# Attention and two MLPs: matmuls with the same stationary operand placed next to each other

## The chip, the cores and the metric

The kernel runs on one core of a Trainium2 chip. The metric is the device time in microseconds (us) of one execution. Matmuls run on TensorE (PE; its weight loads are shown as PEld). VectorE is DVE, ScalarE is ACT, GpSimd is POOL and SyncE is SP. A matmul holds one operand in the array, the stationary one, which a weight load brings there, and streams the other, the moving one, past it.

## The reference

2304 tokens go through top-k attention and then through two MLPs with the same shapes (512 to 2048 to 512) and other activations. Cut to what matters:

```python
def _attn_ref(q, k, v):              # 4 batches, 8 heads, 576 positions, 64 wide
    scores = scale * np.matmul(q, k.transpose(0, 1, 3, 2))
    kth = np.partition(scores, -32, axis=-1)[..., -32:-31]
    scores = np.where(scores >= kth, scores, -1000000000.0)
    attn = np.exp(scores - np.max(scores, axis=-1, keepdims=True))
    attn = attn / (np.sum(attn, axis=-1, keepdims=True) + 1e-09)
    return np.matmul(attn, v)

x = attn_out.transpose(0, 2, 1, 3).reshape(2304, 512)
h = x @ w_in;  y = (h - np.tanh(h)) @ w_out              # first MLP
h = y @ w_in2; g = np.where(h > 0, h, np.exp(np.minimum(h, 0)) - 1)
out = g @ w_out2                                         # second MLP
```

## The kernel before

The tokens are cut into 6 chunks (`ci`) of 384. The attention of a later chunk runs while the MLPs of an earlier one run, so PE has matmuls of both. For the attention, PE makes scores (L383, L384: two matmuls that share their stationary operand `u.qs`), ACT copies them out (L385), and DVE finds the 32nd largest of each row of 576 in four rounds: MAX8 (L406) finds eight, MATCH_REPLACE (L420) takes them out, and after the last round a mask (L427) is applied. PE then transposes the result (L448) and multiplies it with v (L470).

An MLP (`m` is 0 for the first and 1 for the second) goes over 16 f-tiles (`ft`), each 128 of the 2048 hidden features. Every float32 operand is split into a high and a low part, and a product is the sum of three: high by high, and high by low both ways.

- `first(ci, m, ft)` makes 12 matmuls into the bank `h` (L577): the stationary operand is one of four blocks (`kt`) of the high (`wi` 0) or low (`wi` 1) weights `wt`, the moving one `xh` or `xl`, 384 columns. For `m` 1 the same roles are played by `zh` and `zl`, and the first two f-tiles (`PARTED`) are made in two column parts, 256 and 128 wide. ACT makes `t` from `h` (L580; L582 and L583 for `m` 1). There are two `h` banks, so `first` of f-tile ft+2 waits until the gate has read the bank of f-tile ft.
- `gate` makes `g` from `h` and `t`, on DVE (L591 for `m` 1, L596 for most f-tiles of `m` 0), and splits it: ACT makes `gh`, POOL `gl` (both L148 and L149, in a helper).
- `second(ci, m, ft)` adds nine matmuls to the three `acc` banks (L613), one for each 128 tokens `t`: the stationary operand is `gh[t]` or `gl[t]`, the moving one the high or low weights, 512 columns.
- `between(ci)` is the turn from the first MLP to the second: for each 128 tokens ACT copies `acc` to `y` (L627), PE transposes it (L630), ACT makes `zh` (L632) and DVE `zl` (L633). `first` of the second MLP's f-tiles 0 and 1 follows at once.

Every engine works through its own queue in order. The order is fixed when the kernel is built: the Python code emits the steps tick by tick, so many rounds of the attention beside so many f-tiles, and a list scheduler then places each instruction by its priority and a simulated time. A change in one engine's order can thus move instructions on the others.

Of the kernel before, what the change touches and what calls it, by code (L numbers as in the profile page):

```python
# [106 lines left out]
def tile_topk_attention_two_mlps(  # L107
# [20 lines left out]
    def mlp_tile(shape, dt, **kw):  # L128
        if "open" in pools:
            opening.close()  # L130
            del pools["open"]
            pools["mlp"] = pool("mlp", 1)
        return pools["mlp"].tile(shape, dt, **kw)
# [23 lines left out]
    def bank(tag, name, bufs):  # L157
        if tag == "h":
            if "park" in pairs:
                turns.close()  # L160
                del pairs["park"]
                pairs["h"] = pool("ph", 1, PSUM)
            return pairs["h"].tile([P, 512], F32, tag=tag, name=name, bufs=bufs)
        return ps.tile([P, 512], F32, tag=tag, name=name, bufs=bufs)
# [401 lines left out]
    def first(ci, m, ft):  # L566
        n = SIZES[ci]
        xh, xl = x_tiles[ci] if m == 0 else z_tiles[ci]
        h = bank("h", f"h{ci}_{m}_{ft}", 2)[:, :n]
        wv = weights[ci, m, ft][:, 0].rearrange("p a (k c) -> p a k c", c=P)  # L570
        jobs = [(wi, xs, kt) for wi, xs in ((0, xh), (1, xh), (0, xl)) for kt in range(4)]
        if m == 0 and ft == 0:
            jobs.sort(key=lambda x: x[2])
        late = (n // P - 1) * P
        for cs in (slice(0, late), slice(late, n)) if m == 1 and ft < PARTED and late else (slice(0, n),):
            for a, (wi, xs, kt) in enumerate(jobs):
                nc.tensor.matmul(h[:, cs], wv[:, wi, kt], xs[:, kt, cs], start=(a == 0), stop=(a == len(jobs) - 1))  # L577
        t = mlp_tile([P, NMAX], F32, tag="t", name=f"t{ci}_{m}_{ft}", bufs=T_BUFS)[:, :n]
        if m == 0:
            nc.scalar.activation(t, h, AF.Tanh)  # L580
        else:
            nc.scalar.activation(t, h, AF.Relu, scale=-1.0)  # L582
            nc.scalar.activation(t, t, AF.Exp, scale=-1.0)  # L583
        parts[ci, m, ft] = h, t
# [17 lines left out]
    def second(ci, m, ft):  # L602
        nt = SIZES[ci] // P
        if ft == 0:
            acc[ci, m] = [bank(f"acc{t}", f"acc{ci}_{m}_{t}", 1) for t in range(nt)]
        wt = weights.pop((ci, m, ft))[:, 1]
        gh, gl = parts.pop((ci, m, ft))
        jobs = [(k, t) for k in range(3) for t in range(nt)]
        if ft == NF - 1:
            jobs.sort(key=lambda x: x[1])  # L610
        for k, t in jobs:
            gx, wi = ((gh, 0), (gh, 1), (gl, 0))[k]
            nc.tensor.matmul(  # L613
                acc[ci, m][t],
                gx[:, t * P : t * P + P],
                wt[:, wi],
                start=(ft == 0 and k == 0),
                stop=(ft == NF - 1 and k == 2),
            )
# [31 lines left out]
    def step_parts(i):  # L651

        ci, m, ft = steps[i]
        nxt = steps[i + 1] if i + 1 < len(steps) else None
        turn = m == 0 and ft == NF - 1
        early = nxt is not None and not turn

        def a():
            if early:
                first(*nxt)  # L660

        def b():
            if early:
                gate(*nxt)

        def c():
            second(ci, m, ft)
            if turn:
                between(ci)
                first(*nxt)  # L670
                gate(*nxt)
            if m == 1 and ft == NF - 1:
                store(ci)
            load_next()

        return a, b, c
# [54 lines left out]
    for tick in range(FIRST_TICK, n_ticks):  # L731
# [7 lines left out]
        if tick == starts[0]:  # L739
            first(*steps[0])  # L740
            gate(*steps[0])
# [71 lines left out]
```

## Time and profile before

| | |
|---|---|
| time, median of 3 runs | 1217.33 us (1217.17 to 1217.76) |
| time of the profiled execution | 1221.19 us |
| its span | 1219.4 us |
| busy in the span: PE, PEld | 1150.4 us (94%), 976.2 us (80%) |
| busy in the span: DVE, ACT, POOL | 950.1 us (78%), 764.1 us (63%), 503.1 us (41%) |
| matmuls, weight loads | 6349, 6349 |
| mean granted clock of PE | 0.972 of full speed |

The span is the stretch between the first and the last recorded instruction; the time of an execution also holds what lies around it. Rows of the trace and sums of them belong to the profiled execution.

### The profile page before, as it was taken

The page shows a single profiled execution, that of the slowest core. Times are in us where ns is not written, and L with a number is a line of the kernel's source. Part 1 is how long each engine was busy: PE and PEld are TensorE (multiplying, and loading weights), DVE is VectorE, ACT ScalarE, POOL GpSimd, SP SyncE. Part 2 cuts the span into 40 slices and gives each one's busy share as a digit, 9 for nine tenths or more (in the row PEclk, how much of TensorE's full clock was granted, in tenths as well). Part 3 has the DMA queues.
Part 4 walks back from the last instruction along what each step waited for, and adds up shares of the span by engine and source line. Part 5 has one row for each costly group of instructions (what it writes and reads, how often), then busy time and mean ns, then how long its engine had stood idle before and what let it go on. Part 6 is the DMA issues. An engine that isn't in the chain of part 4 may idle for free.

```text
span 1219.4 us, 18848 instructions
## 1 busy us (share of the span) xinstructions
PE 1150.4 (94%) x6349; PEld 976.2 (80%) x6349; DVE 950.1 (78%) x1896; ACT 764.1 (63%) x1592; POOL 503.1 (41%) x557
## 2 busy tenths in 40 slices
PE   6477789998999999999999999999999999999998
PEld 3344478887887978898988988988988988898897
DVE  7899999998999999789888779898789996100111
ACT  4999978988975546474564666575555564432333
POOL 2345348666752323253524444434434413333221
PEclk9688899998999999999999999999999999999999
DMA  7999728984989985759886779988679875686572
GB/s 233 361 354 336 241 73 295 365 288 142 385 345 290 288 302 144 246 162 315 251 187 206 238 239 247 226 243 271 218 248 221 205 154 207 210 285 247 195 270 95
DMA packets 81328, 299.59 MB, mean 246 GB/s; under 512 B 18768, under 2 KB 36048, under 8 KB 51664
## 3 DMA queue, kind: packets, MB, share of 16 engines
q1 hardware_dynamic: 81232, 298.39, 76.8%
q8 instruction: 50, 0.82, 0.3%
q14 instruction: 46, 0.38, 0.1%
HBM read 252.97 MB, written 45.39 MB: 245 GB/s over the span
## 4 chain that ended last, share of the span: by engine, by line
PE 58%; ACT 2%; DVE 1%; POOL 0%; issue 0%; ACTq 0%; POOLq 0%; DVEq 0%
PE acc L613 24%; PE h L577 24%; PE av L470 3%; PE pt L448 3%; PE ps L383 2%; PE ps L384 2%; DVE vm L406 0%; ACT y L627 0%; DVE w L420 0%; ACT zh L632 0%; ACT e L410 0%; ACT ph L449 0%; ACT s L385 0%; POOL kk L149 0%; ACT t L583 0%
## 5 line engine op out<-in xcount | busy, mean ns | idle before, releaser
L149 POOL TENSOR_TENSOR gl<-g,gh 128x384 fp32r<-128x384 f32 x192 | 203.4, 1061 | 371.8 <-ACT gh L148 352.3
L406 DVE MAX8 vm<-w 128x8 f32<-128x576 f32 x432 | 315.8, 748 | 3.2
L613 PE MATMUL acc<-wt,gh 128*128 128x512 f32 x1002 | 267.2, 398 | 0.3 <-ACT gh L148 0.3
L420 DVE MATCH_REPLACE8 w<-vm,w 128x576 f32<-128x576 f32 x288 | 212.8, 740 | 0.0
L613 PEld LDWEIGHTS acc<-wt,gh 128*128 128x128 f32 x1002 | 183.7, 188 | 33.9 <-issue 2.7
L148 ACT ACTIVATE gh<-g 128x384 fp32r<-128x384 f32 x192 | 100.6, 526 | 83.8 <-DVE g L591 43.3
L591 DVE SCALAR_TENSOR_TENSOR g<-t,h 128x384 f32<-128x384 f32 x96 | 52.4, 545 | 127.8 <-ACT t L583 127.4
L577 PE MATMUL h<-zh,wt 128*128 128x384 f32 (+2 forms) x768 | 145.8, 326 | 2.4 <-ACT zh L632 1.2
L613 PE MATMUL acc<-wt,gl 128*128 128x512 f32 x501 | 146.4, 398 | 0.0
L577 PE MATMUL h<-xh,wt 128*128 128x384 f32 x664 | 140.0, 339 | 2.0 <-DVE g L591 1.2
L448 PE MATMUL pt<-ident,e 128*116 128x128 f32 (+1 forms) x720 | 117.8, 290 | 20.2 <-ACT e L423 8.3
L385 ACT ACTIVATE s<-ps 128x288 f32<-128x288 f32 (+1 forms) x272 | 106.8, 416 | 45.2 <-PE ps L384 36.6
L406 DVE MAX8 vm<-s 128x8 f32<-128x576 f32 x144 | 107.4, 751 | 34.6 <-ACT s L385 32.6
L577 PEld LDWEIGHTS h<-zh,wt 128*128 128x128 f32 x768 | 124.9, 190 | 8.8 <-ACT zh L632 2.4
L449 ACT ACTIVATE ph<-pt 116x384 f32<-116x384 f32 (+1 forms) x240 | 111.2, 500 | 30.0 <-PE pt L448 29.5
L448 PEld LDWEIGHTS pt<-ident,e 128*116 128x116 f32 (+1 forms) x720 | 90.4, 143 | 43.2 <-ACT e L423 11.4
L577 PEld LDWEIGHTS h<-xh,wt 128*128 128x128 f32 x664 | 116.2, 188 | 9.0 <-DVE g L591 1.5
L582 ACT ACTIVATE t<-h 128x384 f32<-128x384 f32 x96 | 46.7, 488 | 108.2 <-PE h L577 108.0
L613 PEld LDWEIGHTS acc<-wt,gl 128*128 128x128 f32 x501 | 92.1, 188 | 18.5
L420 DVE MATCH_REPLACE8 w<-vm,s 128x576 f32<-128x576 f32 x144 | 106.6, 741 | 0.0
L580 ACT ACTIVATE t<-h 128x384 f32<-128x384 f32 x96 | 47.0, 491 | 90.9 <-PE h L577 90.8
L596 DVE TENSOR_TENSOR g<-h,t 128x384 f32<-128x384 f32 x76 | 41.4, 546 | 72.0 <-ACT t L580 71.5
(82 smaller groups left out, 1958.3 us busy)
## 6 DMA issues: line engine op xcount, KB each, us to landing
wt<-w SPq DMA_DIRECT2D x167, 1024.0 KB, 6.0
wr<-in_w_dram SPq DMA_DIRECT2D x32, 1024.0 KB, 8.9
w<-wp SPq DMA_DIRECT2D x32, 1024.0 KB, 8.4
kraw<-in_kT_dram SPq DMA_DIRECT2D x96, 144.0 KB, 5.4
vraw<-in_vL_dram SPq DMA_DIRECT2D x64, 160.0 KB, 5.2
sd<-sp SPq DMA_DIRECT2D x24, 288.0 KB, 5.8
s<-sd SPq DMA_DIRECT2D x24, 288.0 KB, 8.9
qraw<-in_qT_dram SPq DMA_DIRECT2D x64, 96.0 KB, 5.6
```

Source lines behind the costliest of these rows:

```text
L148: nc.scalar.activation(hi, src, copy)
L149: return nc.gpsimd.tensor_sub(lo, src, f(hi))
L385: nc.scalar.activation(s[lo:hi, cs], pt[lo:hi, :HS], copy)
L406: nc.vector.max(g.vm[:, j, min(r, 1)], u.s[t] if r == 0 else g.w[j])
L420: nc.vector.match_replace(g.w[j], v, u.s[t] if r == 0 else g.w[j], FILL)
L448: nc.tensor.transpose(pt[:kn, j * P : j * P + P], v.e[t][:, k0 : k0 + kn], ident)
L449: nc.scalar.activation(g.ph[:kn, blk, :nq], pt[:kn, :nq], copy)
L577: nc.tensor.matmul(h[:, cs], wv[:, wi, kt], xs[:, kt, cs], start=(a == 0), stop=(a == len(jobs) - 1))
L580: nc.scalar.activation(t, h, AF.Tanh)
L582: nc.scalar.activation(t, h, AF.Relu, scale=-1.0)
L591: nc.vector.scalar_tensor_tensor(g, t, -1.0, h, op0=ALU.add, op1=ALU.max)
L613: nc.tensor.matmul(acc[ci, m][t], gx[:, t * P : t * P + P], wt[:, wi], start=(ft == 0 and k == 0), stop=(ft == NF - 1 and k == 2),)
```

## The change

In `first`, the twelve matmuls of an f-tile are sorted so that the one with `xh` and the one with `xl` on the same block of high weights stand next to each other; the four on low weights come last. Before, the four with `xl` stood last. Only f-tile 0 of the first MLP had been sorted by `kt`. In `second`, `gh[t]` is used for the high and for the low weights in a row, and the three `gl` come last, as before; f-tile 15 already had the pairs.

```diff
         h = bank("h", f"h{ci}_{m}_{ft}", 2)[:, :n]
         wv = weights[ci, m, ft][:, 0].rearrange("p a (k c) -> p a k c", c=P)
-        jobs = [(wi, xs, kt) for wi, xs in ((0, xh), (1, xh), (0, xl)) for kt in range(4)]
+        jobs = [(wi, xs, kt) for wi, xs in ((0, xh), (0, xl), (1, xh)) for kt in range(4)]
         if m == 0 and ft == 0:
             jobs.sort(key=lambda x: x[2])
+        else:
+            jobs.sort(key=lambda x: (x[0], x[2]))
...
         jobs = [(k, t) for k in range(3) for t in range(nt)]
         if ft == NF - 1:
             jobs.sort(key=lambda x: x[1])
+        else:
+            jobs.sort(key=lambda x: (x[0] == 2, x[1]))
         for k, t in jobs:
             gx, wi = ((gh, 0), (gh, 1), (gl, 0))[k]
```

No instruction is added or taken away, and each engine has as many as before. Their order is another on every engine, because the scheduler places them anew. After the change two lines stand between, so L591 is L593, L577 is L579, L630 is L634 and L633 is L637.

On DVE, at the turn of chunk 1, the row that matters is the first gate of the second MLP, `g_1_0`. Names beginning with `w_`, `vm_` and `s_` are the top-k's work tiles, its maxima and the scores of one head and 128 rows. Before, it is row 623 of DVE's order, and these rows lead up to it:

```order
L406 MAX vm_3_2_3_1_192_0_4954<-w_3_2_3_1_192_0_2_4959 128x8
L406 MAX vm_3_2_3_1_192_1_5226<-w_3_2_3_1_192_1_0_5229 128x8
L406 MAX vm_3_2_3_1_192_1_5226<-w_3_2_3_1_192_1_1_5230 128x8
L420 MATCH_REPLACE w_3_2_3_1_192_0_2_4959<-vm_3_2_3_1_192_0_4954,w_3_2_3_1_192_0_2_4959 128x576
L591 SCALAR_TENSOR_TENSOR g_1_0_4834<-t_1_0_4831,h_1_0_4806 128x384
```

After the change it is row 638, and the rows ahead of it belong to later rounds of the next group:

```order
L406 MAX vm_3_2_3_1_192_1_5226<-w_3_2_3_1_192_1_1_5230 128x8
L420 MATCH_REPLACE w_3_2_3_1_192_1_0_5229<-vm_3_2_3_1_192_1_5226,w_3_2_3_1_192_1_0_5229 128x576
L406 MAX vm_3_2_3_1_192_1_5226<-w_3_2_3_1_192_1_2_5231 128x8
L420 MATCH_REPLACE w_3_2_3_1_192_1_1_5230<-vm_3_2_3_1_192_1_5226,w_3_2_3_1_192_1_1_5230 128x576
L406 MAX vm_3_2_3_1_192_1_5226<-w_3_2_3_1_192_1_0_5229 128x8
L420 MATCH_REPLACE w_3_2_3_1_192_1_2_5231<-vm_3_2_3_1_192_1_5226,w_3_2_3_1_192_1_2_5231 128x576
L593 SCALAR_TENSOR_TENSOR g_1_0_4834<-t_1_0_4831,h_1_0_4806 128x384
```

So 15 instructions that stood behind this gate now stand ahead of it: 7 MAX8, 7 MATCH_REPLACE and one mask (L427). Nothing that stood ahead of it has moved behind it. On PE, what stands ahead of `first` of f-tile 2 of that MLP, which waits for this gate, has grown by 9 transposes (L448) and 8 score matmuls (L383, L384). By f-tile 9 of the first MLP of chunk 2 the gate has the same row in DVE's order as before.

On PE, at the turn of chunk 5, which has no attention left beside it, the rows are these before:

```order
L630 MATMUL yt_2_12502<-ident,y_2_12484 128x128 x4
L577 MATMUL h_1_0_12509<-zh_12480,wt_1_0_12339 128x256 x8
L577 MATMUL h_1_1_12545<-zh_12480,wt_1_1_12372 128x256 x8
L577 MATMUL h_1_0_12509<-zl_12481,wt_1_0_12339 128x256 x4
L577 MATMUL h_1_0_12509<-zh_12480,wt_1_0_12339 128x128 x8
```

And these after:

```order
L634 MATMUL yt_2_12502<-ident,y_2_12484 128x128 x4
L579 MATMUL h_1_0_12509<-zh_12480,wt_1_0_12339 128x256
L579 MATMUL h_1_1_12545<-zh_12480,wt_1_1_12372 128x256
L579 MATMUL h_1_0_12509<-zl_12481,wt_1_0_12339 128x256
L579 MATMUL h_1_0_12509<-zh_12480,wt_1_0_12339 128x256
L579 MATMUL h_1_0_12509<-zl_12481,wt_1_0_12339 128x256
...
L579 MATMUL h_1_0_12509<-zh_12480,wt_1_0_12339 128x256 x4
```

The first matmul that needs `zl` had 16 matmuls with `zh` ahead of it and now has 2. The turns of the other chunks have the same two job lists with matmuls of the attention among them.

## Rows read from the trace of the kernel before

**Rows 1.** The page, busy time by engine: us, share of the span, instructions.
```profile
PE 1150.4 (94%) x6349; PEld 976.2 (80%) x6349; DVE 950.1 (78%) x1896; ACT 764.1 (63%) x1592; POOL 503.1 (41%) x557
```

**Rows 2.** Busy us by engine in stretches of the span; then clock, DMA share, GB/s.
```profile
core 0: us, PE busy (x) PEld busy (x) DVE busy (x) ACT busy (x) POOL busy (x), PEclk, DMA share, GB/s
275.00:280.00 5.00, 2.29 (x10) 1.30 (x9) 4.90 (x11) 4.93 (x13) 0.23 (x1) 0.73 0.67 267
290.00:360.00 70.00, 69.12 (x432) 59.12 (x432) 65.21 (x112) 61.15 (x113) 49.70 (x41) 1.00 0.86 318
360.00:440.00 80.00, 78.82 (x428) 66.79 (x427) 78.51 (x167) 37.80 (x78) 26.22 (x45) 1.00 0.94 289
440.00:500.00 60.00, 58.34 (x345) 50.65 (x344) 60.00 (x131) 38.85 (x86) 18.22 (x26) 1.00 0.71 228
500.00:520.00 20.00, 20.00 (x107) 16.15 (x106) 11.06 (x21) 6.51 (x14) 4.89 (x6) 1.00 0.68 228
```

**Rows 3.** Chain of waits that ended last, 451 to 520: start, us, what.
```profile
453.26 1.99 DVE vm L406 x3
...
459.07 1.46 DVE w L420 x2
...
464.63 0.55 DVE g L591
...
513.91 2.09 PE h L577 x12
```

**Rows 4.** PE's timeline at 465: start, us, operation, in brackets idle time before, releaser.
```profile
465.22 1.66 PE L577 MATMUL h<-zh,wt 128*128 128x384 f32 x8 [0.76 <-DVE g L591]
```

**Rows 5.** PE's timeline, f-tiles 14 and 15 of chunk 5's first MLP.
```profile
1138.62 1.56 PE L613 MATMUL acc<-wt,gh 128*128 128x512 f32 x6
1140.02 0.86 PE L613 MATMUL acc<-wt,gl 128*128 128x512 f32 x3
1140.72 1.56 PE L613 MATMUL acc<-wt,gh 128*128 128x512 f32 x6
1142.12 0.86 PE L613 MATMUL acc<-wt,gl 128*128 128x512 f32 x3
```

**Rows 6.** PE's timeline, score matmuls at 910.
```profile
909.73 0.30 PE L383 MATMUL ps<-kk,qs 128*128 128x288 f32 x1
909.87 0.30 PE L384 MATMUL ps<-kk,qs 128*128 128x288 f32 x1
910.00 0.29 PE L383 MATMUL ps<-kk,qs 128*128 128x288 f32 x1
```

**Rows 7.** PE's timeline, turn of chunk 5.
```profile
1145.16 2.15 PE L577 MATMUL h<-zh,wt 128*128 128x256 f32 x16 [0.32 <-ACT zh L632]
...
1151.27 0.96 PE L577 MATMUL h<-zh,wt 128*128 128x384 f32 x4 [0.39 <-DVE g L591]
```

**Rows 8.** DVE's timeline, turn of chunk 5.
```profile
1144.65 1.89 DVE L633 TENSOR_TENSOR zl<-yt,zh 128x512 fp32r<-128x512 f32 x3 [6.72 <-ACT zh L632]
```

**Rows 9.** PE's timeline, turns of chunks 2 and 4.
```profile
629.54 2.15 PE L577 MATMUL h<-zh,wt 128*128 128x256 f32 x16 [0.20 <-ACT zh L632]
...
631.80 0.49 PE L448 MATMUL pt<-ident,e 128*116 128x128 f32 x3
632.04 0.72 PE L577 MATMUL h<-zl,wt 128*128 128x256 f32 x4
...
637.17 0.40 PE L383 MATMUL ps<-kk,qs 128*128 128x288 f32 x1 [0.37 <-ACT ph L449]
...
993.07 2.15 PE L577 MATMUL h<-zh,wt 128*128 128x256 f32 x16 [0.20 <-ACT zh L632]
```

**Rows 10.** DVE's timeline, turns of chunks 2 and 4.
```profile
630.60 1.27 DVE L633 TENSOR_TENSOR zl<-yt,zh 128x512 fp32r<-128x512 f32 x2
...
994.12 1.27 DVE L633 TENSOR_TENSOR zl<-yt,zh 128x512 fp32r<-128x512 f32 x2
```

**Rows 11.** PE's timeline, after the turn of chunk 0.
```profile
277.74 0.61 PE L383 MATMUL ps<-kk,qs 128*128 128x288 f32 x1 [2.28 <-ACT s L385]
```

## The prediction

> **What bounds the kernel now.** I read the page first. PE is busy 94% of the span and DVE 78% [rows 1], so a matmul saved or a PE wait added moves the end. The same row counts one weight load for each matmul, pairs that share a stationary operand included. Then I read the stretches, because 94% is a mean [rows 2]: from 290 to 440 PE is short of full by 0.9 and 1.2 us, while DVE is idle 4.8 and 1.5 us; from 440 to 500 DVE is busy 60.00 of 60 us and PE is the one that gives way; from 500 on PE has no gap and DVE is idle 9 of 20 us. The chain of waits says the same: through 451 to 465 us it runs along DVE, over MAX8 and MATCH_REPLACE, to the gate L591, and then goes back to PE and stays there [rows 3]. At 465.22 PE has waited 0.76 us for that gate [rows 4]. So this is a PE-bound kernel in which, at the turn of chunk 1, DVE sets the pace for a while. It is the one place where the order of DVE's queue decides when PE goes on.
>
> **Term A, the pairs themselves: 0.** The order shows 738 new pairs in `first` and 522 in `second` with the same stationary operand. The kernel before has such pairs already. F-tile 14 of the first MLP has the old order and f-tile 15 the paired one; start to start, the six `gh` matmuls take 1140.02 - 1138.62 = 1.40 us in f-tile 14 and 1142.12 - 1140.72 = 1.40 us in f-tile 15, so 0.233 us each in both [rows 5]. The score matmuls L383 and L384 share `u.qs`: from L383 to L384 with the same stationary operand 0.14 us, from L384 to the next L383 with another one 0.13 us [rows 6]. Starts are shown to 0.01 us, so six matmuls with three pairs could hide 0.01 us, 0.0033 us a pair: 1260 pairs by 0.0033 us bound the term by 4 us on either side. I take 0, to which both rows come nearest. The Trainium skill says otherwise in one respect: its page "TensorE: Matmul & The Clock Gate", section "Step-by-step: what each phase is for", describes the weight load as separate so that one load can serve many matmuls, which would make a paired second matmul cheaper, but it also says that the next weights load while a matmul runs. By the first sentence the pairs save time, by the second nothing; the equal 1.40 us of the two f-tiles agrees with the second. What is left of the change is then what the new orders do to waits.
>
> **Term B, the turn of chunk 1: +4.4 us.** On DVE, 15 top-k instructions have moved ahead of the gate `g_1_0`, and nothing has moved behind it. One MAX8 takes 1.99 / 3 = 0.66 us, one MATCH_REPLACE 1.46 / 2 = 0.73 us in the chain [rows 3]; the mask I price as a MATCH_REPLACE, which reads as many elements. That is 7 x 0.66 + 7 x 0.73 + 0.73 = 10.5 us. PE, which waits for this gate with `first` of f-tile 2, has only 9 transposes and 8 scores more to do ahead of it: 9 x 0.08 (three in 632.04 - 631.80 = 0.24 us [rows 9]) + 8 x 0.133 [rows 6] = 1.8 us. PE waits there already [rows 4], so nothing else covers it, and the gate would be up to 10.5 - 1.8 = 8.7 us later as PE sees it. Behind that wait stand all of PE's later matmuls. They are late with it, because from 500 on PE is 20.00 of 20 us busy [rows 2] and can't catch up. That is the upper bound, for a DVE with no time to spare ahead of the turn. The lower bound is 0: the top-k work is the same in sum, and DVE has 4.8 + 1.5 = 6.3 us idle between 290 and 440 [rows 2], in which the moved rounds may run if their scores are there. Whether they are, the trace of before does not show. I take the middle, 4.4 us: the 6.3 us of idle time are spread over 150 us, each a wait for an input, and not all can be filled. Less than a third filled would leave 8.7 - 2.1 = 6.6 us, all of it 2.4 us.
>
> **Term C, the turn of chunk 5: +0.5 us.** Before, PE has 16 `zh` matmuls ahead of the first `zl` one; they run 2.15 us from 1145.16 on [rows 7] and cover DVE's `zl`, of which the second of three is done at about 1144.65 + 2 x 0.63 = 1145.9 [rows 8]. After the change only two stand ahead, at 2.15 / 16 = 0.13 us each, so PE asks for `zl` at 1145.16 + 0.27 = 1145.43 and stands for 0.5 us. What the 14 other `zh` matmuls covered is now uncovered, and they run afterwards. Nothing gives it back: PE's next wait, 0.39 us at 1151.27 [rows 7], is for a gate that starts from the same matmuls and is late with them.
>
> **Term D, the same at the turns of chunks 2, 3 and 4: +1.0 us.** At chunk 2, `zl` of the first 256 columns is there at 630.60 + 0.63 = 631.23 [rows 10]; PE would come to it at 629.54 + 0.27, with two scores (0.27) and three transposes (0.24) between [rows 9], at 630.3: 0.9 us. At chunk 4 it is there at 994.12 + 0.63 = 994.75 [rows 10], and PE, with nine transposes and two scores between, would be there at 993.07 + 0.27 + 0.27 + 0.72 = 994.33: 0.4 us. Chunk 3 lies between, 0.65; together 2.0 us. Some of that falls into waits that follow (0.37 us at 637.17 [rows 9]), where PE waits for ACT and would wait less. I take half, 1.0 us, with 0 and 2.0 as ends.
>
> **The turn of chunk 0: 0.** There `zl` is late too, by some 2 us at 16 against 2 matmuls, but PE then waits 2.28 us for score copies of ACT at 277.74 [rows 11], which hides it. If that cover were gone, it would cost up to 1.7 us.
>
> **Sum.** 0 + 4.4 + 0.5 + 1.0 = 5.9 us. The profiled execution took 1221.19 us, 0.3% over the median of the runs, 1217.33 us; from its own time the sum gives 1227.1 us, and from the median, which is what is timed, 1217.33 + 5.9 = 1223.2 us.
>
> **Rivals.** Faster or slower means by more than 0.2%, 2.4 us, which is about what a measurement can tell: below 1214.9 or above 1219.8 us.
>
> *The clock falls at the new stall.* After the 2.28 us wait at 277.74 [rows 11], the granted clock from 275 to 280 is 0.73 of full [rows 2], a mixture of PE's two levels of 2.4 and 1.2 GHz. If the stall of term B came in one piece of several us, PE could run some us at 1.2 GHz behind it. From 275 to 280 a share of 0.27 x 2 x 5 = 2.7 us lies at the lower level, and half of that speed is lost: 1 to 3 us more on a stall of full size, 8.7. That gives 1217.33 + 8.7 + 1.5 + 2 = about 1229 us (1225 to 1231). Against it: the stall may come in pieces, with transposes and scores between them.
>
> *Hidden.* If the moved top-k rounds fit into DVE's 6.3 us of idle time and the rest of the 10.5 us (10.5 - 6.3 - 1.8 = 2.4 us) is partly met by the 0.76 us PE waits now, terms B to D come to 1 to 2 us: 1218 to 1219, no change to be told. For it: the scheduler moved these rounds ahead because in its simulated time their inputs are there. Against it: DVE's 60.00 of 60 us.
>
> *Faster by the weights.* The second matmul of a pair is spared its load. The rows price it two ways. With 288 columns a matmul takes 0.133 us, with 512 columns 0.233 us, so by a line through both there is a fixed part of about 5 ns; sparing it 1260 times saves 6 us, 1211 us. Or the matmul goes down to its columns at 2.4 GHz: 512 columns 213 ns against 233, 384 columns 160 against 2.09 / 12 = 174 ns [rows 3]; 522 x 20 + 738 x 14 ns = 21 us, 1196 us. It decides as soon as a pair saves more than 5.9 / 1260 = 5 ns. Against it: 1.40 us in both f-tiles [rows 5]. The sentence of the Trainium skill on one load for many matmuls is this rival's rule, and the rows of this case speak against it.
>
> *Faster by earlier top-k.* The moved rounds run earlier, so the masked rows are ready earlier, and PE waits less for the attention: 2.28 us at 277.74 and the 0.9 + 1.2 us missing from 290 to 440 [rows 2, 11] sum to 4.4 us, about 1213 us if all goes. It decides if DVE's moved work runs entirely in idle time. Against it: these waits are for ACT and gates, not for a mask.
>
> **How the numbers follow.** The forecast, slower by 2.5 to 10 us with terms B to D, gets 0.55; the clock 0.15; hidden 0.17; the weights 0.05; earlier top-k 0.08. So slower is 0.55 + 0.15 = 0.70, same 0.17, faster 0.13. That the change does not do what it says, with as many loads as before, is part of the forecast, not a rival. The predicted time is that of the forecast, 1223.2 us; its own range is 1219.8 (B at 2.4 us less than chosen, D at 0) to 1228 (B at 8.7, C, D at 1.5). The whole range reaches down to 1215.5, which takes in the hidden case and leaves out most of the two faster ones (0.12), and up to 1230, which leaves out the end of the clock's (0.04).
>
> **What would show it.** Term A: PEld still at 6349, the six `gh` at 1.40 us in every f-tile, 384 columns at 0.174 us. Term B: at the turn of chunk 1 PE waits several us for L593 where it waited 0.76, with MAX8 and MATCH_REPLACE in the chain ahead, and all that follows is later by as much, still at 520 us. Term C and D: a PE wait for DVE L637 of 0.4 to 0.9 us at four turns. If 384-column matmuls start less than 0.17 us apart within a pair, term A was wrong, and the time falls by more than all other terms. If L593 is on time, term B was, and the sum is left at 1.5 us, no change. Clock: a granted clock under 1.00 between 465 and 480.

## The result, and the profile after

The changed kernel takes 1230.57 us (median of 4 runs, 1230.27 to 1233.73) against 1217.39 us before: the ratio is 1.0116, 95% interval 1.0103 to 1.0128. It is 13 us slower, where 1223.2 us (1215.5 to 1230.0) was forecast. The profiled execution took 1230.27 us with a span of 1228.5 us. That is 0.3 us under its median. The kernel before was profiled 3.8 us over its own median; a second profile of it (e1) has a span of 1218.4 us. So the two spans differ by 10.1 us, and these are what the traces can explain. The other 3 us are no more than the spread of the runs of before, which took 1214 to 1224 us over all experiments; no trace shows them.

The page of the changed kernel has the same work as [rows 1], with as many weight loads as matmuls:

```profile
PE 1148.6 (93%) x6349; PEld 974.7 (79%) x6349; DVE 951.3 (77%) x1896; ACT 763.7 (62%) x1592; POOL 506.1 (41%) x557
```

The stretches that answer to [rows 2] (us of the span, then busy us of each engine, the granted clock, the DMA share and GB/s) are:

```profile
275.00:280.00 5.00, 5.00 (x42) 4.79 (x42) 4.71 (x12) 4.56 (x11) 1.97 (x3) 1.00 0.66 269
290.00:360.00 70.00, 67.42 (x427) 58.51 (x426) 65.77 (x114) 60.38 (x112) 50.94 (x46) 1.00 0.86 306
360.00:440.00 80.00, 79.44 (x435) 67.43 (x434) 79.61 (x170) 39.32 (x84) 24.89 (x41) 1.00 0.91 310
440.00:500.00 60.00, 55.56 (x309) 47.07 (x308) 60.00 (x130) 34.68 (x77) 17.10 (x27) 0.94 0.60 186
500.00:520.00 20.00, 20.00 (x106) 16.10 (x105) 11.25 (x23) 8.87 (x18) 6.19 (x7) 1.00 0.62 206
```

From 440 to 500 us PE is busy 2.8 us less than before, and its clock is 0.94 where it was 1.00: 0.06 x 60 = 3.6 us of PE time at full clock. At 275 us, where before PE stood and then ran at the lower level, it now is busy throughout.

To see where time is lost for good, I compared the two traces at equal work: each matmul counts with its usual start-to-start time, and the lag is how much later a run has done as much of PE's work as e1 had at a given time. It is worked out from the starts of all 6349 matmuls.

```
lag on e1, us, at          290    440    480    800    820   1140   1210
changed kernel            -0.5    0.2    7.6    7.0    9.2    9.4   10.1
```

So 7.4 us go at the turn of chunk 1, 2.2 at that of chunk 3, and 0.7 at that of chunk 5. PE's timeline at the turn of chunk 1 (start, us, operation, idle time before and its releaser) shows why:

```profile
445.46 1.14 PE L448 MATMUL pt<-ident,e 128*116 128x128 f32 x9
...
449.72 3.45 PE L470 MATMUL av<-ph,vraw 112*64 112x384 f32 x20
...
456.92 1.63 PE L634 MATMUL yt<-ident,y 128*128 128x128 f32 x12 [0.22 <-ACT y L631]
460.85 0.50 PE L579 MATMUL h<-zh,wt 128*128 128x256 f32 x2 [2.30 <-ACT zh L636]
462.10 2.17 PE L448 MATMUL pt<-ident,e 128*116 128x128 f32 x9 [0.74 <-ACT e L423]
464.42 0.61 PE L383 MATMUL ps<-kk,qs 128*128 128x288 f32 x1 [0.15 <-ACT ph L449]
...
474.31 0.44 PE L579 MATMUL h<-zh,wt 128*128 128x384 f32 x1 [0.16 <-DVE g L593]
```

PE waits 2.30 us for zh, then 0.74 for the attention's exponentials, and only 0.16 us for the gate. Nine transposes take 2.17 us where nine took 1.14 us at 445.46, with the clock at 1.00. ACT's timeline has the cause of the first wait:

```profile
457.71 0.62 ACT L636 ACTIVATE zh<-yt 128x512 fp32r<-128x512 f32 x1
458.19 0.80 ACT L422 ACTIVATE e<-s,nk 128x576 f32<-128x576 f32 x1
458.86 1.46 ACT L410 ACTIVATE e<-s,mb 128x576 f32<-128x576 f32 x2
460.19 1.10 ACT L636 ACTIVATE zh<-yt 128x512 fp32r<-128x512 f32 x2
```

Three steps of the attention stand between the first and the second zh: one for the mask (a Prelu, L422) and two exponentials (L410). Where the text and the expectations below speak of three exponentials, these are meant. The clock follows the wait:

```profile
455.00:460.00 5.00, 3.33 (x20) 2.29 (x18) 5.00 (x12) 3.78 (x8) 0.58 (x3) 1.00 0.55 25
460.00:465.00 5.00, 3.26 (x13) 2.64 (x14) 5.00 (x13) 3.16 (x8) 0.23 (x1) 0.66 0.95 310
465.00:470.00 5.00, 5.00 (x33) 5.00 (x31) 5.00 (x11) 0.55 (x2) 0.00 (x0) 0.66 0.51 185
```

And in the kernel before (e1, its second profile) PE has work of the attention at that place, between zh and zl:

```profile
452.43 2.15 PE L577 MATMUL h<-zh,wt 128*128 128x256 f32 x16
454.42 0.82 PE L448 MATMUL pt<-ident,e 128*116 128x128 f32 x6
455.87 3.45 PE L470 MATMUL av<-ph,vraw 112*64 112x384 f32 x20 [0.63 <-ACT ph L449]
...
459.89 0.63 PE L577 MATMUL h<-zl,wt 128*128 128x256 f32 x4
```

There ACT makes the first two zh in a row, with no step of the attention between, and PE does not wait for them:

```profile
451.27 1.11 ACT L632 ACTIVATE zh<-yt 128x512 fp32r<-128x512 f32 x2
```

In the changed kernel those 20 `av` matmuls run ahead of the turn (449.72 above), with transposes and scores beside them.

### The profile page after: what moved, and what is told of

It is laid out like the page before. It is cut to its first block, busy times and chain, and to the rows that moved or that the text cites. A ratio compares the mean times of both kernels' runs of the same rounds, so it can differ in the third digit from the quotient of the medians.

```text
span 1228.5 us, 18839 instructions
## 1 busy us (share of the span) xinstructions
PE 1148.6 (93%) x6349; PEld 974.7 (79%) x6349; DVE 951.3 (77%) x1896; ACT 763.7 (62%) x1592; POOL 506.1 (41%) x557
## 4 chain that ended last, share of the span: by engine, by line
PE 66%; ACT 3%; DVE 1%; issue 0%; POOL 0%; ACTq 0%; DVEq 0%; POOLq 0%
PE acc L617 27%; PE h L579 27%; PE av L470 4%; PE pt L448 4%; PE ps L383 2%; PE ps L384 2%; DVE vm L406 1%; ACT zh L636 1%; ACT y L631 0%; ACT ph L449 0%; ACT e L410 0%; DVE w L420 0%; ACT s L385 0%; POOL kk L149 0%; DVE g L593 0%
## 5 line engine op out<-in xcount | busy, mean ns | idle before, releaser
L149 POOL TENSOR_TENSOR gl<-g,gh 128x384 fp32r<-128x384 f32 x192 | 206.8, 1079 | 357.0 <-ACT gh L148 332.9
L406 DVE MAX8 vm<-w 128x8 f32<-128x576 f32 x432 | 319.1, 750 | 3.4
L579 PE MATMUL h<-zh,wt 128*128 128x384 f32 (+2 forms) x768 | 197.4, 326 | 4.6 <-ACT zh L636 3.5
L579 PE MATMUL h<-xh,wt 128*128 128x384 f32 x664 | 185.6, 340 | 1.0 <-DVE g L598 0.9
L593 DVE SCALAR_TENSOR_TENSOR g<-t,h 128x384 f32<-128x384 f32 x96 | 52.3, 544 | 126.2 <-ACT t L585 126.2
L579 PEld LDWEIGHTS h<-zh,wt 128*128 128x128 f32 x768 | 136.2, 190 | 11.0 <-ACT zh L636 4.6
L448 PE MATMUL pt<-ident,e 128*116 128x128 f32 (+1 forms) x720 | 114.5, 286 | 29.4 <-ACT e L423 9.1
L448 PEld LDWEIGHTS pt<-ident,e 128*116 128x116 f32 (+1 forms) x720 | 89.0, 141 | 51.0 <-ACT e L423 12.4
L579 PEld LDWEIGHTS h<-xh,wt 128*128 128x128 f32 x664 | 121.0, 188 | 6.2 <-DVE g L598 1.6
L579 PE MATMUL h<-zl,wt 128*128 128x384 f32 (+2 forms) x384 | 121.3, 325 | 1.8 <-DVE zl L637 1.6
L584 ACT ACTIVATE t<-h 128x384 f32<-128x384 f32 x96 | 46.9, 488 | 118.9 <-PE h L579 118.8
L579 PE MATMUL h<-xl,wt 128*128 128x384 f32 x332 | 112.0, 337 | 0.0
```

Source lines behind the costliest of these rows:

```text
L149: return nc.gpsimd.tensor_sub(lo, src, f(hi))
L406: nc.vector.max(g.vm[:, j, min(r, 1)], u.s[t] if r == 0 else g.w[j])
L448: nc.tensor.transpose(pt[:kn, j * P : j * P + P], v.e[t][:, k0 : k0 + kn], ident)
L593: nc.vector.scalar_tensor_tensor(g, t, -1.0, h, op0=ALU.add, op1=ALU.max)
```

## The experiments

Times and ratios (with 95% interval) are against runs of the kernel before on the same chip; its medians there were 1217.4 to 1219.5 us.

```
run                       us        ratio   interval           gate's row, turn 1
the change                1230.57   1.0116  1.0103 to 1.0128   638
e2 second product only    1218.26   0.9991  0.9982 to 0.9999   623
e3 first product only     1231.49   1.0104  1.0091 to 1.0118   638
e4 alternating, unpaired  1233.93   1.0126  1.0109 to 1.0143   639
e5 f-tiles 2 to 15        1219.96   1.0013  1.0001 to 1.0024   623
e6 one f-tile             1229.0    1.0091  1.0075 to 1.0107   635
e7 gate held early        1230.9    1.0102  1.0085 to 1.0119   626
e8 e7, PE kept busy       1227.87   1.0083  1.0067 to 1.0100   626
e9 zh first on ACT        1230.44   1.0086  1.0064 to 1.0109   633
e10 av held back          1230.67   1.0091  1.0074 to 1.0109   633
e11 av and gate           1228.25   1.0076  1.0051 to 1.0101   624
e12 from chunk 1 on       1221.95   1.0022  1.0008 to 1.0035   624
e13 all three waits       1223.84   1.0046  1.0034 to 1.0059   624
e14 before, PE busy       1221.36   1.0017  1.0005 to 1.0029   623
```

### The pairs, or the order they bring (e1 to e6)

**e1** is the kernel before, unchanged.

> The kernel before, unchanged, for a second profile. Its first profiled execution took 1221.2 us where the median of the runs is 1217.4 us, the changed kernel's took its own median, so the spans differ by 9.1 us and the medians by 13.2. If the first profile was 4 us long by a chance wait, this one has a span of about 1215.6 us and the missing 4 us lie before the turn of chunk 1; if the profile itself costs the kernel before 4 us, the span is 1219 us again.

One execution, 1220.2 us, with a span of 1218.4 us: nearer to the second number, and within the 1216.9 to 1221.6 us of the 15 other runs there. It is 1.0 us shorter than the first profile, in two pieces near 460 and 920 us, so no chance wait of 4 us ahead of the turn explains the first. That the profile itself costs 4 us is not shown either, since the changed kernel's did not.

**e2** leaves `first` as it was.

```diff
-        jobs = [(wi, xs, kt) for wi, xs in ((0, xh), (0, xl), (1, xh)) for kt in range(4)]
+        jobs = [(wi, xs, kt) for wi, xs in ((0, xh), (1, xh), (0, xl)) for kt in range(4)]
         if m == 0 and ft == 0:
             jobs.sort(key=lambda x: x[2])
-        else:
-            jobs.sort(key=lambda x: (x[0], x[2]))
```

> The pairs in the second product alone. DVE's order is then that of the kernel before, row for row. Theory 1 (a pair is worth nothing, the time comes from the new order of waits): 1217.4 us within 1.5, six gh matmuls 1.40 us at every f-tile. Theory 2 (every pair costs the same, 13.2 us over 1260 pairs or 10.5 ns): 522 pairs, 1222.9 us, six gh matmuls 1.43 us. Theory 3 (pairs gain and the waits cost more than 13 us): below 1216 us.

Theory 1 holds: 0.09% faster, at the edge of what can be told (the interval ends at 0.9999), and DVE's order did not move by a row. By the lag e2 is 1.2 us ahead of e1 at 290 us and 0.9 us at the end, so the 522 pairs of the second product gain nothing behind that.

**e3** leaves `second` as it was (the two added lines with `x[0] == 2` are taken out).

> The pairs in the first product alone. DVE's order is then that of the changed kernel, row for row, the gate of the turn of chunk 1 in row 638. Theory 1 (order of waits): 1230.5 us within 2, as the whole change. Theory 2 (every pair costs the same): 738 pairs, 1225.1 us.

The whole loss is there, with 738 of the 1260 pairs. Both products of f-tiles in the changed kernel show why the pairs themselves count for nothing:

```profile
477.05 1.56 PE L617 MATMUL acc<-wt,gh 128*128 128x512 f32 x6
478.45 0.34 PE L579 MATMUL h<-zh,wt 128*128 128x384 f32 x1
478.62 0.34 PE L579 MATMUL h<-zl,wt 128*128 128x384 f32 x1
478.80 0.34 PE L579 MATMUL h<-zh,wt 128*128 128x384 f32 x1
...
480.53 0.85 PE L617 MATMUL acc<-wt,gl 128*128 128x512 f32 x3
```

Six paired `gh` matmuls take 478.45 - 477.05 = 1.40 us, as in [rows 5]; the twelve of `first` take 480.53 - 478.45 = 2.08 us against 2.09 in [rows 3], and within a pair the step is 0.17 us (478.45 to 478.62) as it is from one pair to the next (478.62 to 478.80: 0.18).

**e4** alternates `xh` and `xl` as the change does, but each with another block, and takes `gh[t]` apart in the same way.

```diff
             jobs.sort(key=lambda x: (x[0], x[2]))
+            for i in range(0, 8, 2):
+                jobs[i + 1] = (0, xl, (i // 2 + 2) % 4)
...
+            jobs = [(0, 0), (0, 1), (1, 0), (0, 2), (1, 1), (1, 2), (2, 0), (2, 1), (2, 2)]
```

> High and low moving operands alternate in the first product as in the changed kernel, so zl is wanted as early, but no two neighbours share a stationary operand, there or in the second product up to f-tile 14. The gate of the turn of chunk 1 stands in row 639 of DVE's order. Theory 1 (order of waits): slower than before by 8 to 14 us, 1225 to 1231 us, with the loss at the turn of chunk 1. Theory 2 (the pairs cost): 1217 to 1220 us. If pairs gain, it is slower than the changed kernel by more than 2 us.

Almost without new pairs it is as slow; its interval overlaps that of the change, and 7.4 us go from 440 to 480 us. (The f-tiles 0 of the first MLP kept the order of the change, with 24 new pairs of its 1260, which the expectation overlooks.) The loss belongs to the order, not to the pairs.

**e5** pairs the first product in f-tiles 2 to 15 only, **e6** in one f-tile of the whole kernel; both with the new second product.

```diff
+        paired = ft >= 2                      # e6: (ci, m, ft) == (0, 0, 0)
+        rest = ((0, xl), (1, xh)) if paired else ((1, xh), (0, xl))
+        jobs = [(wi, xs, kt) for wi, xs in ((0, xh), *rest) for kt in range(4)]
```

> All new pairs of the second product and those of the first product in f-tiles 2 to 15 of every chunk and MLP; f-tiles 0 and 1 keep the old order. DVE's order is that of the kernel before but for some neighbours that change places, and the gate of the turn of chunk 1 stands in row 623 again. Theory 1 (a pair is worth nothing, the loss is in the order around the turns): 1218 us within 2. Theory 2 (a pair costs, or the denser wants of xl and zl do): more than half of the 13 us, over 1224 us.

> Of the first product only f-tile 0 of chunk 0's first MLP has the new order, 12 matmuls; the second product is paired, which moved nothing on DVE. The scheduler then puts the gate of the turn of chunk 1 into row 635 of DVE's order, 12 behind the kernel before, though nothing at that turn was changed. Theory 1 (what costs is where the scheduler puts the top-k against that gate): slower by 5 to 11 us, 1223 to 1229 us, with the loss at 440 to 500 us. Rival (the early want of zl at the turns costs): 1218 us within 2.

e5 is at the edge of what can be told (0.13%), with most of the pairs in it. e6 costs 0.91% with twelve matmuls of chunk 0 in another order. Its loss is not all at the turn of chunk 1, though, as I had expected: 3.2 us go between 290 and 320 us, 5.7 between 400 and 440, 3.3 between 440 and 480. One early swap moves the attention's order for 250 us. From 400 to 440 us DVE stands 2.92 us for a DMA of scores, and PE then 3.02 us for a gate at 437.80. At the turn of chunk 1, e6 has the `av` matmuls ahead of the turn, as the change has, and the same wait for zh:

```profile
467.26 2.16 PE L581 MATMUL h<-zh,wt 128*128 128x256 f32 x16 [2.30 <-ACT zh L638]
```

But there the granted clock stays at 1.00 from 465 to 475 us, and the turn costs 3.3 us where it costs 7.4 in the change.

### Which wait it is at the turn of chunk 1 (e7 to e13)

**e7** keeps DVE's gate from being overtaken, **e8** adds 24 transposes that fill PE's wait for zh.

```diff
+            done = nc.vector.scalar_tensor_tensor(g, t, -1.0, h, op0=ALU.add, op1=ALU.max)
+            if ft == 0 and ci == 1:
+                newest["turn"] = done
...
+                with behind("turn") if groups[at].id == "2_3_2_3_1_192_1" and r else nullcontext():
                     d()
```

```diff
+        if (ci, m, ft) == (1, 1, 0):          # e8, beside e7's edit
+            for _ in range(24):
+                nc.tensor.transpose(h[:, :P], newest["y"][:, :P], ident)
```

> The changed kernel, but the last three rounds of one top-k group may not be issued ahead of the first gate of chunk 1's second MLP: it comes to row 626 of DVE's order where it stood in 638. PE's and ACT's orders at that turn stay as in the changed kernel but for a few scores. Theory A (DVE's place for the gate alone sets the loss, as term B had it): the 12 rows are worth 8 us, 1222 to 1224 us. Theory B (PE is as late by its own waits for zh and by the lower clock behind them; it waited only 0.16 us for the gate): 1229 to 1231 us.

> As e7, and 24 more transposes of a 128 x 128 tile on PE between the transposes of y and the first zh matmul of chunk 1's turn, into the bank that the next f-tile overwrites: they fill the 2.3 us in which PE waits for zh, and take nothing from other engines. If the granted clock falls because of that wait and its loss is paid in the end, the clock stays at 1.00 from 440 to 500 us and the time is 2 to 4 us under that of e7. If the clock is no part of the loss: as e7 within 1 us, or slower by up to 0.5.

Theory A fell. With the gate 12 rows earlier the time stays. In e7 DVE now idles 4.01 us ahead of the gate, since it waits for `t`, so the gate starts at 473.00 and hardly sooner than in the change (473.71); PE still waits 2.30 us for zh:

```profile
462.86 0.80 PE L579 MATMUL h<-zh,wt 128*128 128x256 f32 x2 [2.30 <-ACT zh L638]
```

```profile
473.00 0.55 DVE L593 SCALAR_TENSOR_TENSOR g<-t,h 128x384 f32<-128x384 f32 x1 [4.01 <-ACT t L585]
```

The clock is a part. The same stretch of e7 and then of e8, each a view by stretches with columns as above:

```profile
440.00:500.00 60.00, 55.30 (x312) 45.40 (x312) 55.23 (x118) 35.68 (x78) 16.73 (x27) 0.94 0.59 178
```

```profile
440.00:500.00 60.00, 57.52 (x341) 48.95 (x340) 56.63 (x123) 35.62 (x78) 17.29 (x28) 1.00 0.62 185
```

From 440 to 480 us e7 loses 7.0 us at equal work, e8 4.8 (its own added work taken out). The medians differ by 3.0 us, with intervals that overlap.

**e9** holds the three exponentials behind the last zh, **e10** holds the `av` matmuls behind the turn's first zh matmul, **e11** is e10 with e7's edit, **e13** is e11 with the old order in the turn's f-tiles 0 and 1.

```diff
+                with behind("zh") if g.id == "2_3_2_3_1_192_1" else nullcontext():  # e9, at L410; L422 alike
                     nc.scalar.activation(u.e[t], u.s[t], AF.Exp, bias=g.mb[:, j : j + 1], scale=SCALE)
...
+            with lift, behind("zmm") if (ci, p) == (2, 2) else nullcontext():  # e10, e11, e13
                 nc.tensor.matmul(
...
+        elif (ci, m) == (1, 1) and ft < PARTED:  # e13
+            jobs.sort(key=lambda x: x[1] is xl)
```

> The changed kernel, but the three exponentials (L410, L422) that ACT works on between its first and second zh copy of chunk 1's turn may only be issued behind the last zh. DVE's gate is in row 633. If the wait for zh starts the loss at that turn (theory B): PE's 2.3 us there shrink to under 0.5 and the clock stays up, 3 to 5 us less than the changed kernel, 1225.5 to 1228 us. If PE then only waits longer for the gate in row 633 (theory A as second limit): under 1.5 us less, 1229 to 1231 us.

> The changed kernel, but the 20 av matmuls of one head pair, which PE did ahead of chunk 1's turn, may only be issued behind the turn's first zh matmul, where the kernel before had them; ACT's exponentials then come behind zh by themselves. The gate is in row 633, 21 rows behind the first zl. If a lack of cover at the turn is the whole loss there: 6 to 7 us less than the changed kernel, 1223.5 to 1225 us. If the gate's place is a second limit of about the same size, PE waits 3 us or more for L596 and the time is 1227 to 1230 us.

> As e10, and the three rounds of top-k held behind the gate as in e7: the gate is in row 624, 12 rows behind the first zl as in the kernel before (13 there). Both limits are lifted: the turn of chunk 1 costs under 2 us and what is left are the later turns, 1220 to 1223.5 us. If the loss at that turn has a third cause, over 1226 us.

> As e11 (av behind the turn's first zh matmul, three rounds of top-k behind the gate), and f-tiles 0 and 1 of chunk 1's second MLP in the old order, so that 16 zh matmuls stand ahead of the first zl one. If the loss at the turn of chunk 1 is these three waits in a row (zh, zl, gate), of which lifting one or two only shows the next: no wait over 1 us and a clock of 1.00 from 440 to 500 us, that turn costs under 1.5 us, and 2 to 3 us of the later turns are left, 1220 to 1223 us. If something else at the turn costs: over 1225 us.

PE's longest waits from 440 to 480 us (us in total, times, longest), first in e9, then in e10, then in e11:

```profile
PE pt L450 <- ACT e L425: 2.7, 1, 2.7
```

```profile
PE h L580 <- DVE zl L640: 2.5, 1, 2.5
```

```profile
PE h L580 <- DVE zl L642: 2.5, 1, 2.5
```

Lifting one wait shows the next. With zh early PE waits 2.7 us for an exponential (L425) that now comes later. With `av` held back ACT makes zh in time too (PE waits 0.32 us for it), but PE waits 2.5 us for zl, because the paired order asks for zl after two matmuls and the scheduler puts `av` behind that (at 463.43 in e10), so that it covers nothing there. So e9, e10 and e11 lose 6.2, 6.6 and 4.8 us from 440 to 480. My expectation for e10 named the gate as its second limit and was wrong in that. Only e13, which has 16 zh matmuls ahead of zl, `av` held back and the early gate, ends it:

```profile
453.19 2.15 PE L582 MATMUL h<-zh,wt 128*128 128x256 f32 x16 [0.32 <-ACT zh L643]
456.13 0.74 PE L582 MATMUL h<-zl,wt 128*128 128x256 f32 x4 [0.79 <-DVE zl L644]
```

```profile
440.00:500.00 60.00, 57.67 (x336) 49.07 (x336) 57.92 (x127) 35.46 (x80) 17.14 (x25) 1.00 0.72 202
```

The turn costs 1.8 us there, the clock stays up, and the lag at the end is 2.9 us, 2.5 of it from the later turns. The median, 1223.84 us, is 0.8 us over what I expected. Whether the early gate is needed beside the other two was not run by itself.

**e12** is the whole change without the first product of chunk 0 (`paired = ci >= 1` in the diff of e5).

> The whole change, but for chunk 0, whose first product keeps the old order. The scheduler then leaves the turn of chunk 1 nearly as in the kernel before: av as cover, the gate in row 624. The new order stands at the turns of chunks 1 to 5, with zl wanted after two matmuls. Terms C and D by themselves: 1.5 us in the sum, as sized by the traces 2.5 to 3: 1219.5 to 1222 us. If the loss belongs to the turn's own new order rather than to the schedule that chunk 0's order brings about: 1226 us or more.

It keeps the `av` matmuls between zh and zl at the turn of chunk 1, although that turn has the new order: it loses 2.3 us there and 2.6 us at the later turns, 3.0 us in all against e1. So most of the loss comes from what chunk 0's new order does to the schedule 200 us later.

### The clock by itself (e14)

The kernel before has a PE wait at the turn of chunk 0 [rows 11] with a low clock behind it. e14 fills it.

```diff
+                    if (u.id, t, half, h) == ("1_3_0_384_0", 1, 1, 0):
+                        for _ in range(18):
+                            nc.tensor.matmul(pt[:, :HS], u.qs[:, qc], u.kh[h][:, cs], start=True, stop=True)
```

> The kernel before, with one score matmul of chunk 0's second-MLP turn (the one ahead of the 2.3 us wait at 277.7) done 18 times more into its own bank, which its last repetition overwrites: PE computes where it stood, and no other engine's order changes. If the clock falls because of the wait and its loss is paid at the end: granted clock 1.00 instead of 0.50 from 278 to 282 us, 2 to 3.5 us less than the kernel before, 1214 to 1216 us where that takes 1217.4, faster than both. If the work that follows only waits for ACT instead: within 1 us of it.

A miss: 0.17% slower, not faster. Stretches of e1 and then of e14:

```profile
278.00:282.00 4.00, 3.48 (x13) 3.02 (x13) 3.89 (x10) 3.88 (x10) 1.65 (x2) 0.50 0.00 0
```

```profile
278.00:282.00 4.00, 3.27 (x13) 3.27 (x14) 3.91 (x8) 3.93 (x7) 1.42 (x1) 0.64 0.00 0
440.00:450.00 10.00, 9.89 (x44) 8.04 (x43) 10.00 (x23) 4.88 (x12) 3.06 (x4) 0.85 0.68 250
```

The lower level was cut short, not avoided: PE still stood 0.56, 0.66 and 0.85 us between 275.6 and 278.73. At equal work without the added one e14 was 4.3 us ahead of e1 at 440 us and 0.8 us ahead at 480. DVE had stood 3.72 us for a DMA of scores (`s<-sd`) and had no gate ready for a PE that came early:

```profile
434.27 1.49 DVE L409 MAX8 vm<-s 128x8 f32<-128x576 f32 x2 [3.72 <-DMA s<-sd]
...
437.72 0.54 DVE L599 TENSOR_TENSOR g<-h,t 128x384 f32<-128x384 f32 x1
...
438.32 1.93 PE L580 MATMUL h<-xh,wt 128*128 128x384 f32 x8 [2.02 <-DVE g L599]
```

PE waited 2.02 us for that gate and ran at a lower clock behind that. In e1 DVE stood only 0.48 us for the scores at that place, and PE not at all. What was won ahead of this place was given back at it and behind it. From 1000 to 1040 us e14 lost another 3.1 us, with a wait of 1.35 us for ACT at 1000.95 and a clock of 0.83 from 1000 to 1010; whether that belongs to the edit is open. Against the expectation, the edit also changed DVE's order, in 265 of its 1365 rows between 278 and 614 us, so e14 does not price the clock by itself. No version that I ran beats the kernel before by more than a measurement can tell; e2, the second product alone, is level with it.

## Why the prediction missed

**Term A** was right: e2 and e4, and the steps above, put the pairs near 0. The two rivals that made it faster are out, since nothing became faster. The weight load was not spared for a single pair (6349 of them as before). The Trainium skill, "TensorE: Matmul & The Clock Gate", section "Step-by-step: what each phase is for", says that weights load while the matmul ahead of them runs. The trace agrees, with 0.17 us from one 384-column matmul to the next, paired or not.

**Term B** had the place and not the wait. It put +4.4 us at the turn of chunk 1, where 7.4 us were lost at equal work. The step that failed is "PE, which waits for this gate with `first` of f-tile 2, has only 9 transposes and 8 scores more to do ahead of it". It took the gate for the one wait of the turn, and looked at what PE had more ahead of f-tile 2, not at where that work stood. The order shows that 20 `av` matmuls moved from between zh and zl to ahead of the turn, and on ACT three exponentials between zh copies; I had read neither row. PE then waited 2.30 us for zh, and 0.16 us for the gate. The gate's lateness was real (473.71 against 464.63 in [rows 3]) but no longer decided anything: PE itself came there late, and in e7, with the gate 12 rows earlier, nothing was gained. The middle of the range was no good choice either: of DVE's 6.3 us of idle time between 290 and 440 the change filled 0.6 + 1.1 = 1.7 us. Nor is this turn the one place where a gate on DVE decides when PE goes on. In the kernel before, PE waits longer for one between 360 and 440 us (line by waits: us in total, times, longest):

```profile
PE h L577 <- DVE g L591: 1.2, 1, 1.2
```

**The clock**, a rival with 0.15, came true, and its time with it (1229 us, 1225 to 1231), but the time in part by luck: it put 8.7 + 2 us at the turn of chunk 1, where stall and clock together cost 7.4, and 1.5 us at the later turns, where 2.9 went; 3 of the 13.2 us stand in no trace. The clock's price here is 3.6 us of PE time, by the granted clock of 0.94 over 60 us; e8, with the clock at 1.00, lost 2.2 us less than e7. I had made it hang on the stall at the gate in one piece, and in the change it came behind that for zh. I gave it too little: [rows 11] show a wait of the same length with the clock low behind it. But it was not sure either, as e6 shows, where the clock stayed up.

**Term C**, +0.5 us at the last turn, was nearly right. PE waits there for zl and then for the gate:

```profile
1154.36 0.39 PE L579 MATMUL h<-zl,wt 128*128 128x256 f32 x1 [0.33 <-DVE zl L637]
...
1160.35 0.44 PE L579 MATMUL h<-zh,wt 128*128 128x384 f32 x1 [0.50 <-DVE g L593]
```

Before, PE had no wait for zl there and 0.39 us for the gate [rows 7]. By the lag, the turn cost 0.7 us.

**Term D**, +1.0 us at the turns of chunks 2 to 4, measured 0.1, 2.2 and 0.1, the last from 980 to 1040 us. The sum of 2.4 is just over its upper end of 2.0, and the wait was another: at chunk 3 PE stood 1.26 us for ACT's copy `xun`, and zl was not waited for.

```profile
815.73 0.87 PE L448 MATMUL pt<-ident,e 128*116 128x128 f32 x6 [1.26 <-ACT xun L484]
```

**The turn of chunk 0** at 0 was not far off, with 1.5 us won in the sum: the changed kernel lost 3.2 us between 250 and 275 us and won 4.7 between 275 and 290, where its clock is 1.00 and not 0.73. PE stood 1.3 us for zl there, as was foreseen.

**Hidden**, one of the rivals, was priced too low: 2.4 - 0.76 = 1.6 us of term B and 1.5 us of C and D make 3.1 us, not 1 to 2.

**What stays open.** The traces explain 10.1 us of 13.2. Why the change moved `av` ahead of the turn is known as far as e12 and e6 go: chunk 0's new order is enough. Which of the scheduler's decisions in between does it was not followed up. Why the clock stayed up in e6 behind a wait of the same length is open too.

## What to carry to other kernels

Where a scheduler places instructions, a reorder that costs nothing in itself is priced by what it does to the order elsewhere: read, on every engine, which work stood between a producer and the one that waits for it, and whether it still stands there. At a turn with several hand-offs in a row (ACT to PE, DVE to PE, gate to PE), the longest wait in the trace is not the price: take the cover away and each hand-off shows, give back one and the next takes its place. A swap that is free in the steady f-tiles should be tried there first, and left out of the turns.

## What the runs showed of the hardware

A wait of PE of 2 us or a little more mostly had the lower clock behind it: 2.28 us at 277.74 before [rows 11], 2.30 us at 460.85 in the changed kernel (0.66 from 460 to 470 us), 2.02 us at 438.32 in e14 (0.85 from 440 to 450 us). But in e6 the same 2.30 us at 467.26 left it at 1.00. Shorter waits went either way: behind 1.35 us at 1000.95 in e14 it was 0.83 from 1000 to 1010 us, and 1.26 us with a shorter wait behind it, at 815.73 in the changed kernel, left it at 1.00. So the length of one wait does not tell whether the clock falls. What the lower level cost was of the order of the wait itself (in the changed kernel 0.34 x 10 = 3.4 us from 460 to 470 us, in e14 0.15 x 10 = 1.5 us), and the time of a stall is the two together.
